# A fused attention, gated feed-forward and spatial-gating kernel: the last token tile made a full, overlapping one, and small attention matmuls given wider streams

## The chip, the cores and the metric

The kernel runs on one core of a Trainium2 chip. The core has a matrix engine (TensorE), a vector engine (VectorE, DVE in the rows), an activation engine (ScalarE, ACT), a general engine (GpSimd, POOL) and a queue engine (SyncE, SP) that starts the transfers between HBM and the core's memory (SBUF). TensorE writes only into PSUM, eight banks of 128 partitions with 512 float32 columns each. The metric is the device time of one launch in microseconds (us).

## The reference

There are three layers behind each other, on 4 batches of 1088 tokens.

1. Linear attention with 4 heads of 32 dimensions. Each q and k row of a head is turned into 64 features: two products with 8x32 matrices S1 and S2 give vectors a and b of 8 numbers, and the features are all products a_i b_j.

```
kv  = einsum('bhsf,bhsd->bhfd', k_p, v);  z = sum(k_p, axis=2)
num = einsum('bhsf,bhfd->bhsd', q_p, kv)
den = einsum('bhsf,bhf->bhs', q_p, z)[..., None] + 1e-06
x   = num / den              # heads side by side: (4, 1088, 128)
```

2. A feed-forward layer with token shift: mixes of x and of x one token earlier go through `w_k` (128x1024), relu and square, then `w_v` (1024x128), times a sigmoid gate from `w_r`.
3. A spatial-gating layer: `w_in` (128x1024) and relu give halves u and v; v is normalised over its 512 features, mixed over tokens by a 1088x1088 matrix plus a bias, multiplied by u, and projected by `w_out` back to 128.

## The kernel before

**Tiling.** The 1088 tokens of a batch are nine tiles: eight of 128 (`NK`) and a last one of 64 (`TAIL`). They are handled in three chunks (`CH`): 384, 384 and 320 tokens, that is three full tiles, three full tiles, and two full tiles with the tail. `rows(t)` gives the rows of a tile. `groups(c)` gives the sets of tiles that one vector instruction can take: one set of three for chunks 0 and 1; for chunk 2 a set of two full tiles and a set with the tail.

**Attention.** `features` (L183) makes three matmuls per chunk, one per tile: the stationary operand is the tile's 128 channels x 128 tokens (64 for the tail), the streamed operand is `Sbd`, a block-diagonal table of 64 columns (4 heads x 16). ScalarE copies the result from PSUM, all of it or the b half, and VectorE or GpSimd forms the 256 products per token (L200 for `KP`, `QP` and batch 1, L208 otherwise). `k_sum` (L217) sums features times v over the nine tiles, for each of two pairs of heads `g`: 128 features stationary, 66 columns streamed (`VP`, two heads of 32 and a column of ones for z). L230 clears the blocks that mix heads with the mask `mk`. `q_turn` (L238) transposes q's features, `q_num` (L255) multiplies them with the masked sums, once per tile and pair, 66 columns streamed into columns of their own, and VectorE divides (L267 to L269). `q_out` (L272) transposes the quotient into `xTs`, and `prep` makes the shifted mixes from it. A plain float32 matmul shows as two instructions in the trace, a float32r matmul and a transpose as one.

**Feed-forward and spatial layer.** `up` (L338) and `down` (L384) run over 96 steps (12 chunks x 8 blocks of 128 hidden features). `mm3` (L108) makes a product from three float32r matmuls of high and low parts with 384 or 320 columns; every second `down` is one plain float32 matmul (L392). `split64` (L119) makes the high and low parts of the weights on VectorE, ScalarE and GpSimd. `v_tile`, `normalise` and `spatial` run the third layer behind it.

**What sets the order.** The program text begins with the weights' and inputs' transfers on SP's queue, 11 warm-up matmuls (L563), the features of k for batch 0, the attention chunk 0 of batch 0, the features and sums of k for batch 1, and then the loop over the 96 steps, in which the other attention chunks are spread by a plan (`plan`, L648; places in `QS`). `behind` issues a call after given instructions; the first weight conversions stand behind the k features and sums (L637, L642), the next behind the first squares of the loop (L693). Inside these bounds a scheduler orders the instructions of each engine by a simulated timeline of its own (L813). Tiles in SBUF and PSUM are shared by name (`sb`, `bank`), so that a transfer into one waits for its last reader: the next v waits for `k_sum`, the next raw weights for a conversion.

Of the kernel before, what the change touches and what calls it, by code (L numbers as in the profile page):

```python
# [21 lines left out]
CH = ((0, 384), (384, 384), (768, 320))  # L22
NCH = len(CH)
NT = 9
NK = 8
TAIL = 64
# [7 lines left out]
VP = 2 * (HD + 1)  # L34
# [28 lines left out]
VW = NH * (HD + 1)  # L63
# [3 lines left out]
def attn_moe_gmlp(ctx: ExitStack, tc: tile.TileContext, qT, kT, va, st, wk, wv, wr, win, wout,  # L67
                  wT, wtail, btail, mu, ident, msk, out):
    nc = tc.nc
    TE, VE, SE, GE = nc.tensor, nc.vector, nc.scalar, nc.gpsimd  # L70
# [16 lines left out]
    def rot(*tags):  # L87
        i = count.get(tags, 0)
        count[tags] = i + 1
        return tags[i % len(tags)]  # L90

    def m(i):
        return f"m{i}"
# [5 lines left out]
        return v if dt == F32 else v.bitcast(dt)  # L99

    idn = sb("idn", [128, 128])
    mk = sb("mk", [128, 8])
    mus = sb("mus", [128, 3])
    half = sb("half", [128, 1])
    ebias = sb("ebias", [128, 1])
# [7 lines left out]
    def copy(dst, src):  # L113
        return SE.activation(out=dst, in_=src, func=AF.Copy)  # L114
# [25 lines left out]
    def flat(r):  # L140
        return r.rearrange("p a b -> p (a b)")
# [8 lines left out]
    def conv64():  # L150
        split64(*pending_raw.pop(0))

    def rows(t):
        return TAIL if t == NT - 1 else 128

    def groups(c):
        return [(0, 3, 128)] if c < 2 else [(0, 2, 128), (2, 1, TAIL)]


    q_s, k_s, v_s, kbd, xTs, kps, qst = {}, {}, {}, {}, {}, {}, {}  # L160
# [13 lines left out]
    def load_v(b):  # L174
        t = sb(rot("xs0H", "xs0L"), [128, NK, NH, HD + 1])
        nc.sync.dma_start(out=t.rearrange("p a b c -> p (a b c)"), in_=va[:, b, :NK * VW])
        t2 = sb(rot("va0", "va1"), [128, NH, HD + 1])
        nc.sync.dma_start(out=t2[:TAIL].rearrange("p b c -> p (b c)"), in_=va[:TAIL, b, NK * VW:])
        v_s[b] = (t, t2)

    outer, k_mask, first = [None], [None], {}

    def features(src, c, dst, pb=4, eng=None, early=False):  # L183
        ab = bank(pb)[:, :192].rearrange("p (t h r) -> p t h r", t=3, h=NH)
        for t in range(3):
            r = rows(3 * c + t)
            TE.matmul(ab[:r, t].rearrange("p h r -> p (h r)"), lhsT=src[:, (3 * c + t) * 128:(3 * c + t) * 128 + r],  # L187
                      rhs=Sbd, start=True, stop=True)
        if eng is None:
            bs = sb(rot("bs0", "bs1"), [128, 3, NH, 8])  # L190
        elif early:
            sab = sb(m(2 + c), [128, 3, NH, 16])
        else:
            sab = sb("sab", [128, 3, NH, 16])
        for t0, n, r in groups(c):
            if eng is not None:
                copy(sab[:r, t0:t0 + n], ab[:r, t0:t0 + n])
                a_ = sab[:r, t0:t0 + n, :, 0:8].rearrange("p t h i -> p (t h) i")
                b_ = sab[:r, t0:t0 + n, :, 8:16].rearrange("p t h j -> p (t h) j")
                outer[0] = eng.tensor_tensor(  # L200
                    out=dst[:r, t0:t0 + n].rearrange("p t (h i j) -> p (t h) i j", h=NH, i=8),
                    in0=a_.unsqueeze(3).to_broadcast([r, n * NH, 8, 8]),
                    in1=b_.unsqueeze(2).to_broadcast([r, n * NH, 8, 8]), op=ALU.mult)
                continue
            copy(bs[:r, t0:t0 + n], ab[:r, t0:t0 + n, :, 8:16])
            a_ = ab[:r, t0:t0 + n, :, 0:8].rearrange("p t h i -> p (t h) i")
            b_ = bs[:r, t0:t0 + n].rearrange("p t h j -> p (t h) j")
            outer[0] = VE.tensor_tensor(  # L208
                out=dst[:r, t0:t0 + n].rearrange("p t (h i j) -> p (t h) i j", h=NH, i=8),
                in0=a_.unsqueeze(3).to_broadcast([r, n * NH, 8, 8]),  # L210
                in1=b_.unsqueeze(2).to_broadcast([r, n * NH, 8, 8]), op=ALU.mult)

    def k_feat(b, c, pb=4, eng=None):
        kp = kps[b, c] = sb((KB1 if b == 1 else ("n0H", "n0L", "n1H"))[c], [128, 3, 256])
# [2 lines left out]
    def k_sum(b, g, ts=range(NT)):  # L217
        if g == 0 and ts[0] == 0:
            kps[b] = bank(3 if b == 1 else 5)
        kv = kps[b]  # L220
        v8 = v_s[b][0].rearrange("p t h c -> p t (h c)")
        v9 = v_s[b][1].rearrange("p h c -> p (h c)")
        for t in ts:
            r = rows(t)
            kp = kps[b, t // 3][:r, t % 3, 128 * g:128 * g + 128]
            vt = (v8[:, t] if t < NK else v9[:r])[:, VP * g:VP * g + VP]
            TE.matmul(kv[:, VP * g:VP * g + VP], lhsT=kp, rhs=vt, start=(t == 0), stop=(t == NT - 1))  # L227
        if g == 1:
            kb = sb(rot("kb0", "kb1"), [128, 2, 2, HD + 1])
            k_mask[0] = VE.tensor_tensor(out=kb, in0=kv[:, :2 * VP].rearrange("p (g h c) -> p g h c", g=2, h=2),  # L230
                             in1=mk[:, 4:6].unsqueeze(1).unsqueeze(3).to_broadcast([128, 2, 2, HD + 1]), op=ALU.mult)
            kbd[b] = kb.rearrange("p g h c -> p g (h c)")

    def q_feat(i):
        qp = qst[i] = sb("n1L", [128, 3, 256])
# [2 lines left out]
    def q_turn(i):  # L238
        c = i % 3
        n = CH[c][1]  # L240
        qp, qt = qst[i], []
        for g in range(2):
            pt = bank(6 + g)
            for t in range(3):
                r = rows(3 * c + t)
                TE.transpose(pt[:, 128 * t:128 * t + r], qp[:r, t, 128 * g:128 * g + 128], idn[:r, :r])  # L246
            q2 = vr(rot(0, 1, 2, 3), CMAX)
            copy(q2[:, :n], pt[:, :n])
            qt.append(q2)
        qst[i] = qt  # L250

    nd_pe, x_copy, x_mu_op = [None], [None], [None]
    nd_last, x_mu, x_turn = [None], [None], [None]

    def q_num(i):  # L255
        b, c = divmod(i, 3)
        qt, kb = qst[i], kbd[b]
        nd = bank(5)[:, :396].rearrange("p (t h c) -> p t h c", t=3, h=NH)
        for t in range(3):
            r = rows(3 * c + t)  # L260
            for g in range(2):
                nd_pe[0] = TE.matmul(nd[:r, t, 2 * g:2 * g + 2].rearrange("p h c -> p (h c)"),  # L262
                                       lhsT=qt[g][:, 128 * t:128 * t + r], rhs=kb[:, g], start=True, stop=True)
        xm = qst[i] = vr(rot(4, 5), CMAX).rearrange("p (t h c) -> p t h c", t=3, h=NH)
        den = sb(rot("de0", "de1"), [128, 3, NH])
        for t0, n, r in groups(c):
            VE.tensor_scalar(out=den[:r, t0:t0 + n], in0=nd[:r, t0:t0 + n, :, HD], scalar1=1e-6, scalar2=None, op0=ALU.add)  # L267
            VE.reciprocal(out=den[:r, t0:t0 + n], in_=den[:r, t0:t0 + n])
            nd_last[0] = VE.tensor_tensor(out=xm[:r, t0:t0 + n], in0=nd[:r, t0:t0 + n, :, 0:HD],  # L269
                             in1=den[:r, t0:t0 + n].unsqueeze(3).to_broadcast([r, n, NH, HD]), op=ALU.mult)  # L270

    def q_out(i):  # L272
        b, c = divmod(i, 3)
        o, n = CH[c]
        if c == 0:
            xTs[b] = sb(f"x{b}", [128, S + 1])
            GE.memset(xTs[b][:, 0:1], 0.0)
        xm = qst.pop(i)
        px = bank(5)
        for t in range(3):  # L280
            r = rows(3 * c + t)
            x_turn[0] = TE.transpose(px[:, 128 * t:128 * t + r], xm[:r, t].rearrange("p h c -> p (h c)"), idn[:r, :r])  # L282
        x_copy[0] = copy(xTs[b][:, 1 + o:1 + o + n], px[:, :n])
        if i == 0:
            a = x_mu[0] = sb(m(1), [128, n])
            x_mu_op[0] = VE.tensor_scalar(out=a, in0=px[:, :n], scalar1=mus[:, 0:1], scalar2=None, op0=ALU.mult)
# [258 lines left out]
        nc.sync.dma_start(out=out[:, b * S + o:b * S + o + n], in_=ob)  # L545


    rawS = sb("rawS", [128, 16, 2], I32)
    nc.sync.dma_start(out=flat(rawS), in_=st.bitcast(I32))
    nc.sync.dma_start(out=mk, in_=msk)  # L550
    load_k(0)
# [10 lines left out]
    for n in range(NWARM):  # L562
# [1 line left out]
    VE.memset(ebias, -896.0 * 2 ** 23)  # L564
    VE.memset(half, -0.5)
    SE.activation(out=warm, in_=half, func=AF.Sigmoid)
    Sl, Ss = sb("Sl", [128, 16]), sb("Ss", [128, 16])
    split64(rawS, 16, None, Sl, Ss)
    Sb = sb("Sbd", [128, NH, 16])
    VE.tensor_tensor(out=Sb, in0=Ss.unsqueeze(1).to_broadcast([128, NH, 16]),  # L570
                     in1=mk[:, 0:NH].unsqueeze(2).to_broadcast([128, NH, 16]), op=ALU.mult)
    Sbd = flat(Sb)
    for t in T2s:
        GE.memset(t.bitcast(F32), 0.0)
# [159 lines left out]
    for b in range(B):  # L734
# [3 lines left out]
        for u, (d, c) in enumerate(order):  # L738
# [78 lines left out]
```

## Time and profile before

| | us |
|---|---|
| median of 3 runs | 487.64 (486.53 to 490.29) |
| the profiled execution | 486.65 |
| its span in the profile | 484.9 |
| TensorE busy (matmul) | 473.9 (98%) |
| VectorE busy | 238.1 (49%) |
| ScalarE busy | 238.8 (49%) |
| GpSimd busy | 190.3 (39%) |

The chain that ended last is TensorE's for 86% of the span, VectorE's for 7%, transfers' for 2%. The profile counts a matmul from its start until its modelled end; since matmuls are pipelined, the pace of a line is read from the chain of waits (length of a piece over its instructions), not from the duration of one.

### The profile page before, as it was taken

The page shows a single profiled execution, that of the slowest core. Times are in us where ns is not written, and L with a number is a line of the kernel's source. Part 1 is how long each engine was busy: PE and PEld are TensorE (multiplying, and loading weights), DVE is VectorE, ACT ScalarE, POOL GpSimd, SP SyncE. Part 2 cuts the span into 40 slices and gives each one's busy share as a digit, 9 for nine tenths or more (in the row PEclk, how much of TensorE's full clock was granted, in tenths as well). Part 3 has the DMA queues.
Part 4 walks back from the last instruction along what each step waited for, and adds up shares of the span by engine and source line. Part 5 has one row for each costly group of instructions (what it writes and reads, how often), then busy time and mean ns, then how long its engine had stood idle before and what let it go on. Part 6 is the DMA issues. An engine that isn't in the chain of part 4 may idle for free.

```text
span 484.9 us, 7337 instructions
## 1 busy us (share of the span) xinstructions
PE 473.9 (98%) x2754; PEld 448.2 (92%) x2754; DVE 238.1 (49%) x452; ACT 238.8 (49%) x577; POOL 190.3 (39%) x248
## 2 busy tenths in 40 slices
PE   7999999899999999999999999999999999999997
PEld 6998788798898889999999999999999999999996
DVE  3525976878866678455572425532225531221221
ACT  2316578888877687766443613333423342411121
POOL 2243755757546468756333612352202342200000
PEclk8557999999999999999999999999999999999999
DMA  7934210011210000012100000000000000100001
GB/s 225 312 106 130 96 47 0 18 49 50 76 32 18 1 1 0 1 48 77 47 18 17 1 15 0 1 1 1 33 15 1 1 1 0 47 0 1 2 0 46
DMA packets 11971, 18.63 MB, mean 38 GB/s; under 512 B 1760, under 2 KB 10528, under 8 KB 11936
## 3 DMA queue, kind: packets, MB, share of 16 engines
q1 hardware_dynamic: 11936, 18.17, 11.9%
q8 instruction: 21, 0.34, 0.3%
q14 instruction: 14, 0.11, 0.1%
HBM read 15.93 MB, written 2.23 MB: 37 GB/s over the span
## 4 chain that ended last, share of the span: by engine, by line
PE 86%; DVE 7%; DMA 2%; ACT 2%; issue 1%; POOL 1%; SPq 1%; DVEq 0%; ACTq 0%; POOLq 0%
PE p L111 65%; PE p L227 5%; PE p L392 4%; PE p L187 3%; PE p L262 2%; DVE w L117 2%; PE p L246 2%; PE p L514 2%; PE p L515 2%; DMA w<-in_qT_dram 1%; PE p L282 1%; DVE w L128 1%; DVE w L124 1%; DMA st<-in_btail_dram 1%; DVE mx L320 1%
## 5 line engine op out<-in xcount | busy, mean ns | idle before, releaser
L519 DVE TENSOR_TENSOR m<-p,m 128x384 f32<-128x384 f32 (+1 forms) x43 | 22.9, 533 | 97.0 <-PE p L515 92.8
L111 PE MATMUL p<-m,k 128*128 128x384 f32 (+1 forms) x288 | 67.5, 353 | 0.4 <-ACT m L114 0.3
L349 POOL TENSOR_TENSOR m<-m 128x384 f32<-128x384 f32 (+1 forms) x48 | 42.2, 884 | 43.6 <-ACT m L346 40.2
L506 ACT ACTIVATE m<-p 128x384 f32<-128x384 f32 (+1 forms) x44 | 20.6, 469 | 77.9 <-PE p L111 76.3
L111 PEld LDWEIGHTS p<-m,k 128*128 128x128 f32 x288 | 49.1, 193 | 3.7 <-ACT m L114 0.5
L111 PE MATMUL p<-w,m 128*128 128x384 f32 (+1 forms) x288 | 52.1, 328 | 0.0
L111 PE MATMUL p<-w,k 128*128 128x384 f32 (+1 forms) x288 | 51.9, 328 | 0.0
L346 ACT ACTIVATE m<-p 128x384 f32<-128x384 f32 (+1 forms) x96 | 43.2, 471 | 16.8 <-PE p L111 16.1
L111 PE MATMUL p<-w,n1H 128*128 128x384 f32 (+1 forms) x192 | 49.2, 332 | 0.1
L111 PEld LDWEIGHTS p<-w,m 128*128 128x128 f32 x288 | 48.1, 188 | 0.4
L111 PEld LDWEIGHTS p<-w,k 128*128 128x128 f32 x288 | 48.0, 188 | 0.4
L111 PE MATMUL p<-w,n0H 128*128 128x384 f32 (+1 forms) x192 | 48.3, 329 | 0.0
L117 DVE TENSOR_TENSOR m<-m,m 128x384 fp32r<-128x384 f32 (+1 forms) x47 | 26.9, 573 | 32.9 <-ACT m L114 27.2
L117 DVE TENSOR_TENSOR w<-m,w 128x384 fp32r<-128x384 f32 (+1 forms) x44 | 33.8, 780 | 18.8 <-ACT w L378 9.6
L111 PEld LDWEIGHTS p<-w,n1H 128*128 128x128 f32 x192 | 34.3, 188 | 1.7 <-DVE x L519 0.5
L392 PE MATMUL p<-w,wvT 128*128 128x384 f32 (+1 forms) x88 | 34.6, 474 | 0.3 <-POOL wvT L687 0.3
L111 PEld LDWEIGHTS p<-w,n0H 128*128 128x128 f32 x192 | 34.1, 188 | 0.6
L460 POOL TENSOR_SCALAR rs<-mv 128x1 f32<-128x1 f32 x34 | 8.6, 254 | 66.3 <-DVE mv L459 65.3
L454 ACT ACTIVATE VR<-p 128x512 f32<-128x512 f32 x34 | 19.7, 597 | 29.7 <-PE p L111 28.4
L111 PE MATMUL p<-w,n1L 128*128 128x384 f32 (+1 forms) x96 | 31.5, 328 | 0.0
L111 PE MATMUL p<-w,n0L 128*128 128x384 f32 (+1 forms) x96 | 31.5, 328 | 0.0
L458 DVE BATCH_NORM_STATS2 bn<-VR 128x6 f32<-128x512 f32 x34 | 23.2, 686 | 14.3 <-ACT VR L454 14.3
(193 smaller groups left out, 1064.6 us busy)
## 6 DMA issues: line engine op xcount, KB each, us to landing
st<-in_wT_dram SPq DMA_DIRECT2D x16, 192.0 KB, 2.4
w<-in_kT_dram SPq DMA_DIRECT2D x8, 192.0 KB, 3.9
w<-in_qT_dram SPq DMA_DIRECT2D x8, 192.0 KB, 4.1
out_dram<-m SPq DMA_DIRECT2D x8, 192.0 KB, 1.9
st<-in_wT_dram SPq DMA_DIRECT2D x8, 160.0 KB, 2.2
xs0H<-in_va_dram SPq DMA_DIRECT2D x2, 528.0 KB, 7.2
xs0L<-in_va_dram SPq DMA_DIRECT2D x2, 528.0 KB, 5.4
w<-in_wk_dram SPq DMA_DIRECT2D x2, 512.0 KB, 5.8
```

The source lines that it names most:

```text
L111: TE.matmul(out_ap, lhsT=l, rhs=r, start=first and n == 0, stop=last and n == 2)
L117: return eng.tensor_tensor(out=L, in0=src, in1=H.bitcast(F32), op=ALU.subtract)
L187: TE.matmul(ab[:r, t].rearrange("p h r -> p (h r)"), lhsT=src[:, (3 * c + t) * 128:(3 * c + t) * 128 + r], rhs=Sbd, start=True, stop=True)
L227: TE.matmul(kv[:, VP * g:VP * g + VP], lhsT=kp, rhs=vt, start=(t == 0), stop=(t == NT - 1))
L246: TE.transpose(pt[:, 128 * t:128 * t + r], qp[:r, t, 128 * g:128 * g + 128], idn[:r, :r])
L346: SE.activation(out=r, in_=hk, func=AF.Relu)
L349: anchor[2] = GE.tensor_tensor(out=sq, in0=r, in1=r, op=ALU.mult)
L392: TE.matmul(vvs[i], lhsT=wvT[:, f // 2], rhs=hls.pop(g), start=f == 0, stop=f == NF - 1)
L454: SE.activation(out=v, in_=pv, func=AF.Relu)
L458: VE.bn_stats(out=bn, in_=v)
L506: SE.activation(out=u, in_=pu, func=AF.Relu)
L519: VE.tensor_tensor(out=u, in0=acc, in1=u, op=ALU.mult)
```

## The change

The last token tile of a batch becomes a full one: it holds the last 128 tokens, 64 of which its neighbour holds too. `cut` gives its place; where transposes write it into a shared PSUM row, `order3` lets it go first, so that its neighbours write over the overlap. In the k sums the rows of the overlap are zero in the v tail (now 128 rows, the values in the last 64), and so is their column of ones. All chunks thus take one instruction per step on VectorE, ScalarE and GpSimd, and `rows` and `groups` go. `Sbd` gets 128 columns, the second 64 of them zero (its mask columns are zero), so that a feature matmul streams 128; the next tile's matmul writes over these. For batches 0 and 2 `k_sum` streams all 132 columns of v for each pair, the mask clears what mixes heads, and `q_num` adds the two pairs up in PSUM with 132 columns each; batches 1 and 3 keep 66. Three small tiles move into shared ones (`rawS`, `Sl`, `Ss`).

```diff
-    mk = sb("mk", [128, 8])
+    mk = sb("mk", [128, 24])
...
+    def order3(c):
+        return (2, 0, 1) if c == NCH - 1 else (0, 1, 2)
+
+    def cut(c, t, o=0):
+        a = CH[c][1] - 128 if t == 2 else 128 * t
+        return slice(o + a, o + a + 128)
...
-        nc.sync.dma_start(out=t2[:TAIL].rearrange("p b c -> p (b c)"), in_=va[:TAIL, b, NK * VW:])
+        nc.sync.dma_start(out=t2.rearrange("p b c -> p (b c)"), in_=va[:, b, NK * VW:])
...
     def features(src, c, dst, pb=4, eng=None, early=False):
-        ab = bank(pb)[:, :192].rearrange("p (t h r) -> p t h r", t=3, h=NH)
+        wide = bank(pb)
+        ab = wide[:, :192].rearrange("p (t h r) -> p t h r", t=3, h=NH)
         for t in range(3):
-            r = rows(3 * c + t)
-            TE.matmul(ab[:r, t].rearrange("p h r -> p (h r)"), lhsT=src[:, (3 * c + t) * 128:(3 * c + t) * 128 + r],
-                      rhs=Sbd, start=True, stop=True)
+            TE.matmul(wide[:, 64 * t:64 * t + 128], lhsT=src[:, cut(c, t, CH[c][0])], rhs=Sbd, start=True, stop=True)
...
+            copy(sab, ab)
...
+        outer[0] = (eng or VE).tensor_tensor(
+            out=dst.rearrange("p t (h i j) -> p (t h) i j", h=NH, i=8),
+            in0=a_.unsqueeze(3).to_broadcast([128, 3 * NH, 8, 8]),
+            in1=b_.unsqueeze(2).to_broadcast([128, 3 * NH, 8, 8]), op=ALU.mult)
...
+        wide = b % 2 == 0
+        w = VW if wide else VP
         for t in ts:
-            r = rows(t)
-            kp = kps[b, t // 3][:r, t % 3, 128 * g:128 * g + 128]
-            vt = (v8[:, t] if t < NK else v9[:r])[:, VP * g:VP * g + VP]
-            TE.matmul(kv[:, VP * g:VP * g + VP], lhsT=kp, rhs=vt, start=(t == 0), stop=(t == NT - 1))
+            kp = kps[b, t // 3][:, t % 3, 128 * g:128 * g + 128]
+            vt = v8[:, t] if t < NK else v9
+            TE.matmul(kv[:, w * g:w * g + w], lhsT=kp, rhs=vt if wide else vt[:, VP * g:VP * g + VP],
+                      start=(t == 0), stop=(t == NT - 1))
...
-            for t in range(3):
-                r = rows(3 * c + t)
-                TE.transpose(pt[:, 128 * t:128 * t + r], qp[:r, t, 128 * g:128 * g + 128], idn[:r, :r])
+            for t in order3(c):
+                TE.transpose(pt[:, cut(c, t)], qp[:, t, 128 * g:128 * g + 128], idn)
...
-                nd_pe[0] = TE.matmul(nd[:r, t, 2 * g:2 * g + 2].rearrange("p h c -> p (h c)"),
-                                       lhsT=qt[g][:, 128 * t:128 * t + r], rhs=kb[:, g], start=True, stop=True)
+                wide = b % 2 == 0
+                o = nd[:, t] if wide else nd[:, t, 2 * g:2 * g + 2]
+                nd_pe[0] = TE.matmul(o.rearrange("p h c -> p (h c)"), lhsT=qt[g][:, cut(c, t)], rhs=kb[:, g],
+                                     start=not wide or g == 0, stop=not wide or g == 1)
...
+    Sb = sb("Sbd", [128, 2 * NH, 16])
+    VE.tensor_tensor(out=Sb, in0=Ss.unsqueeze(1).to_broadcast([128, 2 * NH, 16]),
+                     in1=mk[:, 0:2 * NH].unsqueeze(2).to_broadcast([128, 2 * NH, 16]), op=ALU.mult)
```

## Rows read from the trace of the kernel before

**Rows 1.** The page, the span in 40 slices: TensorE's busy tenths, its granted clock.

```profile
PE   7999999899999999999999999999999999999997
PEclk8557999999999999999999999999999999999999
```

**Rows 2.** Stretches: length; busy us per engine; then granted clock, DMA share, GB/s.

```profile
12.00:24.00 12.00, 12.00 (x55) 11.52 (x55) 6.54 (x14) 4.53 (x11) 2.75 (x2) 0.50 0.94 313
48.00:60.00 12.00, 11.06 (x66) 9.01 (x66) 11.02 (x20) 7.05 (x18) 9.16 (x8) 1.00 0.29 94
```

**Rows 3.** The same table, fine, around the clock's two edges.

```profile
9.40:9.60 0.20, 0.00 (x0) 0.00 (x0) 0.00 (x0) 0.00 (x0) 0.00 (x0) 0.56 1.17 407
43.20:43.40 0.20, 0.20 (x3) 0.08 (x2) 0.08 (x1) 0.20 (x1) 0.20 (x1) 0.50 0.00 0
43.40:43.60 0.20, 0.20 (x2) 0.20 (x2) 0.08 (x1) 0.20 (x2) 0.20 (x1) 0.60 0.00 0
```

**Rows 4.** Timeline: start, length, engine, instruction, idle time before it and its releaser.

```profile
9.88 1.54 PE L187 MATMUL p<-Sbd,w 128*128 128x64 f32 x6 [2.25 <-DMA w<-in_qT_dram]
```

**Rows 5.** Chain of waits, low clock: start, length, line, instructions.

```profile
11.43 3.54 PE p L227 x16
...
16.25 4.85 PE p L227 x20
21.10 1.47 PE p L246 x6
22.57 2.44 PE p L187 x12
25.00 2.76 PE p L262 x12
...
30.32 0.64 PE p L282 x3
30.96 6.88 PE p L227 x30
37.84 2.86 PE p L111 x8
```

**Rows 6.** Chain of waits, full clock: the same lines, and the gated matmul.

```profile
65.72 0.66 PE p L246 x6
66.38 0.65 PE p L187 x6
...
69.77 1.29 PE p L262 x12
...
94.09 1.51 PE p L227 x14
...
103.20 0.65 PE p L392 x2
```

**Rows 7.** Timeline of GpSimd, ScalarE and VectorE between 24 and 42 us.

```profile
24.26 3.11 POOL L200 TENSOR_TENSOR w<-m 128x768 f32<-128x768 f32 x3 [5.05 <-ACT m L114]
...
32.91 0.52 ACT L114 ACTIVATE m<-mx 128x384 fp32r<-128x384 f32 x1 [1.42 <-DVE mx L306]
...
41.80 0.42 DVE L124 TENSOR_SCALAR w<-w 128x512 int32<-128x512 int32 x1
```

**Rows 8.** Batch 0's v: its issue on SP; transfers with us to landing.

```profile
4.00 0.43 SPq L176 DMA_DIRECT2D xs0H<-in_va_dram  x1
...
xs0H<-in_va_dram SPq DMA_DIRECT2D x2, 528.0 KB, 7.2
```

**Rows 9.** Lines by form: tail matmuls, count, busy us, mean ns.

```profile
L187 PE MATMUL p<-Sbd,w 128*64 128x64 f32 x16 | 2.9, 270 | 0.0
...
L262 PE MATMUL p<-kb,VR 128*64 128x66 f32 x16 | 2.2, 240 | 0.0
```

**Rows 10.** Timeline of VectorE, tail instructions of one chunk.

```profile
47.82 0.41 DVE L208 TENSOR_TENSOR n1L<-p,bs 64x256 f32<-64x256 f32 x1
...
60.17 0.28 DVE L269 TENSOR_TENSOR VR<-p,de 64x128 f32<-64x128 f32 x1
```

More of the change, by code (lines that the diff above doesn't have):

```diff
@@ L151, in conv64 @@
         split64(*pending_raw.pop(0))
[L153 to L157, printed above, removed]
+    def order3(c):
[3 more added lines that the diff above has]
+        return slice(o + a, o + a + 128)
     q_s, k_s, v_s, kbd, xTs, kps, qst = {}, {}, {}, {}, {}, {}, {}
@@ L189, in features @@
         if eng is None:
             bs = sb(rot("bs0", "bs1"), [128, 3, NH, 8])
-        elif early:
-            sab = sb(m(2 + c), [128, 3, NH, 16])
-        else:
[L194 to L211, printed above, removed]
@@ new lines, in features @@
+            copy(bs, ab[:, :, :, 8:16])
+            a_ = ab[:, :, :, 0:8].rearrange("p t h i -> p (t h) i")
+            b_ = bs.rearrange("p t h j -> p (t h) j")
+        else:
+            sab = sb(m(2 + c) if early else "sab", [128, 3, NH, 16])
+            copy(sab, ab)
+            a_ = sab[:, :, :, 0:8].rearrange("p t h i -> p (t h) i")
+            b_ = sab[:, :, :, 8:16].rearrange("p t h j -> p (t h) j")
+        outer[0] = (eng or VE).tensor_tensor(
+            out=dst.rearrange("p t (h i j) -> p (t h) i j", h=NH, i=8),
+            in0=a_.unsqueeze(3).to_broadcast([128, 3 * NH, 8, 8]),
+            in1=b_.unsqueeze(2).to_broadcast([128, 3 * NH, 8, 8]), op=ALU.mult)
@@ L222, in k_sum @@
         v9 = v_s[b][1].rearrange("p h c -> p (h c)")
+        wide = b % 2 == 0
+        w = VW if wide else VP
         for t in ts:
-            r = rows(t)
-            kp = kps[b, t // 3][:r, t % 3, 128 * g:128 * g + 128]
-            vt = (v8[:, t] if t < NK else v9[:r])[:, VP * g:VP * g + VP]
-            TE.matmul(kv[:, VP * g:VP * g + VP], lhsT=kp, rhs=vt, start=(t == 0), stop=(t == NT - 1))
+            kp = kps[b, t // 3][:, t % 3, 128 * g:128 * g + 128]
+            vt = v8[:, t] if t < NK else v9
+            TE.matmul(kv[:, w * g:w * g + w], lhsT=kp, rhs=vt if wide else vt[:, VP * g:VP * g + VP],
+                      start=(t == 0), stop=(t == NT - 1))
         if g == 1:
[L229 to L232, printed above, removed]
+            nh = w // (HD + 1)
+            kb = sb(f"kb{b % 2}", [128, 2 * nh, HD + 1])
+            k_mask[0] = VE.tensor_tensor(out=kb, in0=kv[:, :2 * w].rearrange("p (h c) -> p h c", c=HD + 1),
+                                         in1=(mk[:, 8:16] if wide else mk[:, 16:20]).unsqueeze(2)
+                                         .to_broadcast([128, 2 * nh, HD + 1]), op=ALU.mult)
+            kbd[b] = kb.rearrange("p (g h) c -> p g (h c)", g=2)
     def q_feat(i):
@@ L259, in q_num @@
         for t in range(3):
-            r = rows(3 * c + t)
             for g in range(2):
-                nd_pe[0] = TE.matmul(nd[:r, t, 2 * g:2 * g + 2].rearrange("p h c -> p (h c)"),
-                                       lhsT=qt[g][:, 128 * t:128 * t + r], rhs=kb[:, g], start=True, stop=True)
+                wide = b % 2 == 0
+                o = nd[:, t] if wide else nd[:, t, 2 * g:2 * g + 2]
+                nd_pe[0] = TE.matmul(o.rearrange("p h c -> p (h c)"), lhsT=qt[g][:, cut(c, t)], rhs=kb[:, g],
+                                     start=not wide or g == 0, stop=not wide or g == 1)
         xm = qst[i] = vr(rot(4, 5), CMAX).rearrange("p (t h c) -> p t h c", t=3, h=NH)
         den = sb(rot("de0", "de1"), [128, 3, NH])
[L266 to L270, printed above, removed]
+        VE.tensor_scalar(out=den, in0=nd[:, :, :, HD], scalar1=1e-6, scalar2=None, op0=ALU.add)
+        VE.reciprocal(out=den, in_=den)
+        nd_last[0] = VE.tensor_tensor(out=xm, in0=nd[:, :, :, 0:HD],
+                                      in1=den.unsqueeze(3).to_broadcast([128, 3, NH, HD]), op=ALU.mult)
     def q_out(i):
@@ L279, in q_out @@
         px = bank(5)
-        for t in range(3):
-            r = rows(3 * c + t)
-            x_turn[0] = TE.transpose(px[:, 128 * t:128 * t + r], xm[:r, t].rearrange("p h c -> p (h c)"), idn[:r, :r])
+        for t in order3(c):
+            x_turn[0] = TE.transpose(px[:, cut(c, t)], xm[:, t].rearrange("p h c -> p (h c)"), idn)
         x_copy[0] = copy(xTs[b][:, 1 + o:1 + o + n], px[:, :n])
@@ L545, in finish @@
         nc.sync.dma_start(out=out[:, b * S + o:b * S + o + n], in_=ob)
-    rawS = sb("rawS", [128, 16, 2], I32)
+    rawS = sb(m(9), [128, 16, 2], I32)
     nc.sync.dma_start(out=flat(rawS), in_=st.bitcast(I32))
@@ L566, in attn_moe_gmlp @@
     SE.activation(out=warm, in_=half, func=AF.Sigmoid)
-    Sl, Ss = sb("Sl", [128, 16]), sb("Ss", [128, 16])
+    Sl, Ss = sb(m(10), [128, 16]), sb(m(8), [128, 16])
     split64(rawS, 16, None, Sl, Ss)
-    Sb = sb("Sbd", [128, NH, 16])
-    VE.tensor_tensor(out=Sb, in0=Ss.unsqueeze(1).to_broadcast([128, NH, 16]),
-                     in1=mk[:, 0:NH].unsqueeze(2).to_broadcast([128, NH, 16]), op=ALU.mult)
+    Sb = sb("Sbd", [128, 2 * NH, 16])
+    VE.tensor_tensor(out=Sb, in0=Ss.unsqueeze(1).to_broadcast([128, 2 * NH, 16]),
+                     in1=mk[:, 0:2 * NH].unsqueeze(2).to_broadcast([128, 2 * NH, 16]), op=ALU.mult)
     Sbd = flat(Sb)
@@ L776 @@
     va = np.zeros((B, NT * 128, NH, HD + 1), v.dtype)
-    va[:, :S, :, :HD] = v.transpose(0, 2, 1, 3)
-    va[:, :S, :, HD] = 1.0
+    vt = v.transpose(0, 2, 1, 3)
+    va[:, :NK * 128, :, :HD], va[:, :NK * 128, :, HD] = vt[:, :NK * 128], 1.0
+    va[:, -TAIL:, :, :HD], va[:, -TAIL:, :, HD] = vt[:, NK * 128:], 1.0
     wt = moe2_w_spatial.T
@@ L783 @@
     btail[96] = moe2_b_spatial
-    msk = np.zeros((128, 8), np.float32)
+    msk = np.zeros((128, 24), np.float32)
     for h in range(NH):
         msk[32 * h:32 * h + 32, h] = 1.0
-    msk[:64, 4] = 1.0
-    msk[64:, 5] = 1.0
+        msk[64 * (h % 2):64 * (h % 2) + 64, 8 + NH * (h // 2) + h] = 1.0
+        msk[64 * (h % 2):64 * (h % 2) + 64, 16 + h] = 1.0
     host = {
```

## The prediction, made before the changed kernel ran

> **What bounds the kernel now.** I read the row of the granted TensorE clock over the span first. Away from the last slice it is at full speed except in the first tenth [rows 1], and TensorE is busy in nearly every slice. The table of stretches says what that tenth is: from 12 to 24 us TensorE is busy 12.00 of 12.00 us at a granted clock of 0.50, that is at 1.2 instead of 2.4 GHz [rows 2]. The fine table dates the two edges [rows 3]: the clock falls between 9.4 and 9.6 us, with TensorE idle (it waits 2.25 us, to 9.88, for the first chunk of q [rows 4]), and rises between 43.4 and 43.6 us. The reader is to see one low stretch of 34 us, and nothing like it later.
>
> The chain of waits then shows what fills it: TensorE alone, without a pause, on the small float32 matmuls of the first attention steps [rows 5]. A float32 matmul is two instructions here (a features call has 3 matmuls and 6 instructions), so instructions are counted. The feature matmuls (64 columns) take 2.44/12 = 0.203 us each, the sums of k times v (66 columns) 3.54/16 = 0.221, the numerator matmuls (66 columns) 2.76/12 = 0.230. After the rise the same lines take 0.65/6 = 0.108, 1.51/14 = 0.108 and 1.29/12 = 0.108 us [rows 6]. The stretch ends with the first 384-column instructions at 37.84 us [rows 5]; the rise comes 5.7 us behind them. From about 42 us VectorE leads (weight conversions, from the instruction at 41.80 us on [rows 7]; 11.02 of 12.00 us busy in the stretch from 48 [rows 2]), and from about 65 us TensorE again to the end. So time saved ahead of 37.84 us moves all that follows, as long as VectorE's work moves along: its conversions there hang on the first steps of the up projection, and their weights were issued well before.
>
> **The change, part by part.**
>
> *Wider streams, the price.* Feature matmuls go from 64 to 128 streamed columns; the k-v sums and numerators of batches 0 and 2 from 66 to 132; those of batches 1 and 3 stay at 66. The count of instructions does not change. What would 128 columns cost at full clock? The gated 384-column float32 matmul takes 0.65/2 = 0.325 us per instruction, 0.85 ns a column [rows 6], which gives 0.108 for 128 columns and 0.112 for 132: the stream comes out as long as the present pitch, which 64, 66 and 128 columns (the transposes, 0.66/6 = 0.110) all share [rows 6]. I take the pitch of 0.108 to be that of the 128-column stationary load, behind which the stream lies. So 128 columns cost nothing, and 132 cost 4 ns on 144 instructions: 0.6 us, of which about 0.4 lie behind the first stretch. The cover is the stationary load; without it (stream and load one after the other) an instruction would take 0.216. Bounds 0 and 0.108 us each; the transposes, nearest in columns, speak for 0.
>
> *Wider streams, the gain.* The trace shows no 128-column float32 stream of any length while the clock is low, so the effect on the clock is bounded from both sides: none (the clock stays down as now), or never falling. I go by the one rise that the trace shows: 5.7 us after wide instructions began. The wide stream begins again at 9.88 us, so full clock at about 15.6 us. The v data of batch 0 land 7.2 us after their issue at 4.00 us, at 11.2 us, and hold the k-v sum whatever the clock is [rows 8]. Then, from 11.3: 42 instructions (16 and 20 of sums, 6 of features) at 0.221 until 15.6 us makes 19, the other 23 at 0.11 take 2.5 us: 18.1 instead of 21.1 us. Transposes 6 and features 12 at 0.108: 20.05. Numerators, 12: 21.4 instead of 27.8. Then 6 of sums and 6 of features (a repeat of the shapes shown), 3 transposes and 30 narrow sums: 45 x 0.108 = 4.85, up projection from 26.2 instead of 37.84 us: **-11.6 us**. What could be late instead? GpSimd's two feature products of batch 1 take 3.11 us [rows 7]; fed at about 20 us they end at 23.1, and the sums want the last of them at 23.6. The copy that ends the x chain comes 33.43 - 30.96 = 2.5 us after the transposes [rows 5, 7], so 25.5 against 26.2. Both fit by half a microsecond, so an earlier rise is worth little more: with a clock that never falls the sum would end at about 18.1 - 2.2 = 15.9, but GpSimd would hold the up projection to about 24.9, -12.9.
>
> *The first up steps* ran at the low clock: 8 instructions in 2.86 us, half of that back: **-1.4**. The conversions on VectorE start behind them, so this counts too.
>
> *Full tail tile on TensorE.* 16 feature and 16 numerator instructions have 64 stationary columns now [rows 9] and get 128. Between 0 and 0.108 us each, I take half the pitch for half the columns, 0.054: 1.7 us in all, about 1.4 of it behind 26 us where TensorE leads. With the 0.4 above: **+1.8**. The 64-row transposes and sums already load 128 columns: nothing.
>
> *Merged groups on VectorE, ScalarE, GpSimd.* The second instruction of each tail group goes, the first grows. In the stretch that VectorE leads these are a 0.41 us product and a chain that ends with 0.28 us [rows 10]; saved between 0 and 0.7, I take 0.4: **-0.4**. Elsewhere these engines wait for TensorE; nothing. The wider mask product (twice), the mask table of 24 instead of 8 columns and the v tail of 128 instead of 64 rows (33 KB more, four times) stand beside TensorE work or behind the 528 KB of v: nothing; their cover is the work on batch 0 that runs meanwhile, and if it went, 33 KB more would cost 33/528 of those 7.2 us, 0.45 [rows 8].
>
> *Order.* Instructions are ordered by a scheduler's own timeline, which may see wider matmuls as longer and shift some of them. I put +-3 us on it.
>
> Sum: -11.6 - 1.4 + 1.8 - 0.4 = -11.6. The profiled execution took 486.65 us (span 484.9 and 1.75 around it), so 475.0; the median of the runs lies 1.0 above it: **476 us**.
>
> **The rivals.**
>
> *The clock stays down as now.* For it: from 12 to 24 us TensorE was busy all the time, and the clock did not move [rows 2]; no row shows that wide float32 instructions move it. Against it: the one rise followed the change from narrow to wide instructions, and in the mixed stretch from 48 us, with narrow instructions in between, the clock holds at 1.00 [rows 2]. Then only the added terms are left, +1.8 - 0.4 and some 0.4 for four tail instructions at the low clock: 489 us.
>
> The Trainium skill (TensorE: Matmul & The Clock Gate, "What's actually happening") says that the gate follows how busy the engine was lately. If that busy is the busy time of the profile, this change does not touch it and the result is this rival's 489; but the trace disagrees with that reading, since 12.00 busy us of 12.00 left the clock at 0.50.
>
> *The clock rises late, or falls again.* The 30 narrow sums of batch 1 are untouched, 3.2 us of the old kind just ahead of the up projection. If the clock falls in them, the first up steps run slow as now and some of the sums too: -11.6 + 1.8 - 0.4 + 1 = -9.2, 478. If it rises at the numerators (22.6 us) rather than at 15.6, half of the 7 us of delay is lost: 480; a rise at 33 us would leave 485. I put the case at 481.
>
> *Slower: load and stream do not hide each other.* Where the stationary load and a stream of equal length share the array, the pitch may grow. Behind 26 us there are 192 widened instructions (96 feature, 36 sum, 60 numerator), and at 0.216 they cost 192 x 0.108 = +20.7; of the first stretch only the 45 untouched or transposing instructions gain, -4.9, and the first up steps -1.4; with +1.8 - 0.4 that is +15.8: 503. It decides from about 48 ns of growth (some 245 widened instructions at full clock eat 11.7 us), a pitch of 0.156. Against it stands the gated matmul, whose 0.325 has no room for a load in front.
>
> **How the numbers follow.** Forecast 0.60 (own range 471 to 480: the never-falling clock gives 474.7, order and tail terms the rest); late or lost clock 0.19, at 478 to 485; clock down 0.13, at 489; slower 0.08, from 493. Range 471 to 485: the first two cases, 0.79; it leaves out the last two. One per cent, 4.9 us, is about what a measurement of this kernel can tell from no change: faster 0.79, same 0.13, slower 0.08.
>
> **What would show it.** The row of the granted clock should come back to full before 20 us, not at 43 us. The feature lines in the first stretch should go from 0.203 to about 0.11 us, at full clock not over 0.12 for 128 and 132 columns. The first up instruction should stand near 26 us. A clock of 0.50 up to the up projection, or a pitch of over 0.15, would make the forecast wrong; so would an up projection that waits for GpSimd or for a transfer, or conversions on VectorE that do not move forward with it.

## The result, and the profile after

The changed kernel takes 475.4 us (median of 4, 474.82 to 476.61) against 487.29 for the kernel before: a ratio (of the means) of 0.9748, interval 0.9702 to 0.9794. The prediction was 476 us, range 471 to 485. The profiled execution has a span of 473.7 us, 11.2 less.

The page of the changed kernel: busy time of the engines, then the two rows that answer to [rows 1].

```profile
PE 456.4 (96%) x2754; PEld 433.4 (91%) x2754; DVE 235.6 (50%) x433; ACT 236.3 (50%) x569; POOL 189.9 (40%) x247
...
PE   6987999989999999999999999999999999999997
...
PEclk9899999999999999999999999999999999999999
```

The long low stretch is gone: only the second slice shows a dent. TensorE's busy time fell by 473.9 - 456.4 = 17.5 us, more than the span; its idle time (span less busy) rose from 11.0 to 17.3. So 6.3 us of the gain on TensorE were given back as waits. The table of stretches of the changed kernel dates the dent and shows where the waits are (columns as in [rows 2]).

```profile
10.00:12.00 2.00, 1.48 (x11) 1.32 (x12) 0.24 (x2) 0.25 (x1) 0.00 (x0) 0.96 0.99 367
12.00:14.00 2.00, 2.00 (x11) 2.00 (x11) 2.00 (x4) 0.72 (x1) 0.00 (x0) 0.50 1.00 351
14.00:16.00 2.00, 2.00 (x14) 2.00 (x14) 1.93 (x4) 1.06 (x2) 0.00 (x0) 0.69 0.94 315
16.00:18.00 2.00, 2.00 (x21) 2.00 (x20) 0.71 (x3) 0.21 (x2) 1.27 (x1) 1.00 1.04 382
...
30.00:40.00 10.00, 6.87 (x52) 6.26 (x51) 9.23 (x16) 9.28 (x22) 4.62 (x6) 1.00 0.44 131
40.00:50.00 10.00, 8.45 (x50) 6.45 (x49) 8.07 (x14) 4.38 (x12) 6.71 (x7) 1.00 0.28 95
```

From the shares, the clock falls at about 11.8 us and is back at about 15.2, where before it lay low from 9.4 to 43.5 [rows 3]. From 30 to 50 us TensorE is idle for 4.7 of 20 us at full clock while VectorE is busy for 9.23 and 8.07 of 10. The chain of waits of the changed kernel, ahead of the up projection (it answers to [rows 5]):

```profile
11.30 5.97 PE p L219 x36
...
18.43 2.01 DVE w L127
20.46 0.63 ACT w L131
21.09 0.23 ACT m L114
21.32 0.07 issue
21.39 2.98 POOL w L199 x2
24.41 2.89 PE p L219 x24
27.31 1.30 PE p L111 x7
```

The reader is to see that TensorE is no longer alone on it. The sums of batch 0 end at 17.3 us instead of 21.1. Then a conversion step on VectorE took 2.01 us; ScalarE's next conversion step (L131) waited for it, and ScalarE's copy of the batch-1 features stood behind that step in its queue; GpSimd's products started at 21.39, and the k-v sums of batch 1 waited for them until 24.41.

The same stretch in the changed kernel's timeline, TensorE and one VectorE instruction (it answers to [rows 6, 7]):

```profile
18.41 1.50 PE L188 MATMUL p<-Sbd,w 128*128 128x128 f32 x12
...
19.75 1.52 PE L257 MATMUL p<-kb,VR 128*128 128x132 f32 x12
...
21.11 0.83 PE L188 MATMUL p<-Sbd,w 128*128 128x128 f32 x6
...
27.12 1.83 PE L111 MATMUL p<-m,k 128*128 128x384 f32 x9
...
31.27 0.41 DVE L124 TENSOR_SCALAR w<-w 128x512 int32<-128x512 int32 x1
```

From start to start, 12 feature instructions with 128 columns take 19.75 - 18.41 = 1.34 us, 0.112 each; 12 numerator instructions with 132 columns 1.36 us, 0.113 each. The up projection starts at 27.12 instead of 37.77 us (there as here by the start of its first instruction): 10.65 of the span's 11.2 us are won ahead of it.

### The profile page after: what moved, and what is told of

It is laid out like the page before. It is cut to its first block, busy times and chain, and to the rows that moved or that the text cites. A ratio compares the mean times of both kernels' runs of the same rounds, so it can differ in the third digit from the quotient of the medians.

```text
span 473.7 us, 7304 instructions
## 1 busy us (share of the span) xinstructions
PE 456.4 (96%) x2754; PEld 433.4 (91%) x2754; DVE 235.6 (50%) x433; ACT 236.3 (50%) x569; POOL 189.9 (40%) x247
## 4 chain that ended last, share of the span: by engine, by line
PE 71%; DVE 9%; ACT 6%; DMA 5%; POOL 4%; issue 3%; SPq 1%; POOLq 0%; DVEq 0%; ACTq 0%
PE p L111 59%; DMA st<-in_wT_dram 3%; PE p L385 3%; DVE w L117 3%; PE p L219 2%; PE p L257 2%; PE p L507 2%; PE p L508 2%; ACT m L339 2%; DMA xs0H<-in_va_dram 2%; PE p L188 1%; DVE w L127 1%; ACT w L114 1%; DVE m L117 1%; ACT w L371 1%
## 5 line engine op out<-in xcount | busy, mean ns | idle before, releaser
L111 PE MATMUL p<-m,k 128*128 128x384 f32 (+1 forms) x288 | 65.4, 347 | 2.7 <-ACT m L339 2.7
L111 PEld LDWEIGHTS p<-m,k 128*128 128x128 f32 x288 | 47.8, 189 | 6.9 <-ACT m L339 3.7
L455 DVE TENSOR_SCALAR VR<-VR,mv,rs 128x512 f32<-128x512 f32 x34 | 21.1, 621 | 20.4 <-POOL rs L454 20.4
```

The lines of the kernel that those rows point to most:

```text
L111: TE.matmul(out_ap, lhsT=l, rhs=r, start=first and n == 0, stop=last and n == 2)
L455: VE.tensor_scalar(out=v, in0=v, scalar1=mv[:, 0:1], scalar2=rs, op0=ALU.subtract, op1=ALU.mult)
```

## The experiments

"Up" is the start of the up projection, "rest" the span less that; both and TensorE's busy time are from the profiled execution. Ratios are to the kernel before, measured beside each kernel. The profile values of "tail only" stand with its repeat.

| kernel | median us | ratio, interval | up | rest | busy | low clock (start + length, us) |
|---|---|---|---|---|---|---|
| before | 487.3 to 488.2 | | 37.77 | 447.1 | 473.9 | 9.4 + 34.1 |
| changed | 475.4 | 0.9748 (0.9702 to 0.9794) | 27.12 | 446.6 | 456.4 | 11.8 + 3.4 |
| tail only | 489.22 | 1.0042 (1.0009 to 1.0075) | | | | |
| tail only, again | 489.79 | 1.0036 (1.0010 to 1.0061) | 35.65 | 451.8 | 469.6 | 8.1 + 30.7; 59.3 + 3.4 |
| wide only | 484.63 | 0.9917 (0.9887 to 0.9946) | 29.26 | 451.4 | 465.2 | 11.1 + 3.4; 41.9 + 3.4 |
| features only | 478.58 | 0.9801 (0.9757 to 0.9846) | 29.44 | 446.1 | 459.5 | 11.4 + 10.2; 96.7 + 3.4 |
| sums only | 475.81 | 0.9744 (0.9705 to 0.9782) | 27.39 | 447.6 | 457.3 | 8.0 + 6.8; 45.5 + 3.4 |
| before, filled wait | 489.98 | 1.0006 (0.9966 to 1.0046) | 35.23 | 453.5 | 474.1 | 16.2 + 23.9; 91.3 + 3.4 |
| changed, filled wait | 474.11 | 0.9718 (0.9683 to 0.9754) | 27.53 | 445.0 | 457.3 | none |
| early conversion | 475.04 | 0.9734 (0.9701 to 0.9768) | 26.98 | 445.9 | 458.2 | 26.6 + 3.4; 43.6 + 3.4 |
| wide early only | 478.53 | 0.9793 (0.9766 to 0.9820) | 26.37 | 449.8 | 458.6 | 26.2 + 3.4; 94.4 + 3.4 |
| 64-row sums | 476.58 | 0.9761 (0.9733 to 0.9788) | 28.26 | 446.3 | 459.0 | 10.6 + 3.4 |
| all wide | 476.91 | 0.9768 (0.9743 to 0.9793) | 27.33 | 448.3 | 457.3 | 12.2 + 3.4 |
| all three | 475.16 | 0.9731 (0.9706 to 0.9756) | 27.06 | 446.9 | 459.7 | none |

**Which half makes the gain?** Four kernels with parts of the change, first the full tail without wide streams (`tail only`):

```diff
-            TE.matmul(wide[:, 64 * t:64 * t + 128], lhsT=..., rhs=Sbd, start=True, stop=True)
+            TE.matmul(wide[:, 64 * t:64 * t + 64], lhsT=..., rhs=Sbd[:, :64], start=True, stop=True)
...
-        wide = b % 2 == 0        # in k_sum and in q_num
+        wide = False
```

> The change's full tail tile and merged groups, but all streams at 64 and 66 columns as before. Theory A (the gain is the clock, and the clock follows the wide streams): the granted clock stays at 0.50 until the up projection's first matmuls have run for some us, up projection near 37.5 us, time 485 to 489 us. Rival B (the gain is from fewer and merged vector instructions and the order that the scheduler makes of them): 475 to 479 us with the clock low as before.

It took 489.22 us, 0.2 above Theory A's range: the full tail alone gains nothing. The repeat below shows that the clock behaves as before. The wide streams without the full tail (`wide only`; the kernel before, with):

```diff
-            TE.matmul(ab[:r, t].rearrange("p h r -> p (h r)"), lhsT=..., rhs=Sbd, ...)
+            TE.matmul(wide[:r, 64 * t:64 * t + 128], lhsT=..., rhs=Sbd, ...)     # Sbd: 128 columns
...
+        wide = b % 2 == 0        # 132 columns in k_sum and q_num; tail of 64 rows as before
```

> Only the wide streams (128 columns for features, 132 for the sums and numerators of batches 0 and 2); the tail stays 64 rows with instructions of its own. Theory A: clock back at 1.00 by 16 us, up projection near 27 us, 474 to 478 us. Rival B: 484 us or more.

It took 484.63 us, where I expected 474 to 478: a miss, and the time that rival B had named. The clock came back as expected (low for 3.4 us from 11.1), and up moved to 29.26 us, 8.5 earlier, but the rest took 4.3 us longer than before. So the clock theory holds for the first stretch, and the two halves don't add up: +1.8 and -2.8 alone, -11.9 together. On top of the wide streams the full tail, worth nothing alone, is worth 9 us. The tables of stretches from up to the end show where: kernel before, wide only, changed kernel.

```profile
37.77:484.87 447.10, 439.73 (x2603) 415.48 (x2602) 223.85 (x417) 229.56 (x554) 179.63 (x221) 0.99 0.08 24
29.26:480.69 451.43, 442.03 (x2603) 414.47 (x2602) 222.09 (x418) 229.23 (x554) 181.13 (x221) 1.00 0.08 24
27.12:473.74 446.62, 434.09 (x2604) 411.99 (x2603) 219.83 (x401) 227.11 (x548) 179.14 (x221) 1.00 0.08 24
```

Behind up, TensorE is busy for 442.0 us with the small tail and for 434.1 us with the full one; the low stretch at 41.9 us is worth at most 1.7 of these 7.9 us. Then each kind of wide stream by itself, on the changed kernel:

```diff
-        wide = b % 2 == 0
+        wide = False             # features only
```

> The changed kernel with 66 columns for all sums and numerators; only features stream 128. Theory A: of the instructions between 11.3 us and the up projection 66 are features or transposes at best and over 80 are narrow, the 36 sums of batch 0 in one run; the clock falls in that run and comes back late or not before the up projection: 480 to 487 us. If a few wide instructions are enough to hold the clock: 474 to 477. Rival B: 475 to 479.

```diff
-            TE.matmul(wide[:, 64 * t:64 * t + 128], lhsT=..., rhs=Sbd, ...)
+            TE.matmul(wide[:, 64 * t:64 * t + 64], lhsT=..., rhs=Sbd[:, :64], ...)   # sums only
```

> The changed kernel with a table of 64 columns for the features; sums and numerators of batches 0 and 2 stream 132. Theory A: the 36 sums of batch 0 bring the clock back by about 16 us as in the changed kernel; the 12 narrow features behind them (1.3 us) and the narrow sums of batch 1 may lower it again: 474 to 481 us. Rival B: 475 to 479.

478.58 and 475.81 us. The first is below Theory A's range and within rival B's, the second within both. With wide features alone the clock lay low through the 36 narrow sums, for 10.2 us, and up moved to 29.44; with wide sums alone it was low for 6.8 us and up was at 27.39, as in the changed kernel. Either brings most of the gain, with the low stretch shorter where the longest run, the sums, is wide. Fewer vector instructions, the rival, are in all three tail kernels and gain nothing in the first; what they add beside wide streams, these kernels do not separate.

**Why does the full tail alone gain nothing?** The first kernel once more, for its profile.

> The tail-only kernel once more, for its profile: the timed runs gave 489.2 us, 1.8 above before, though its trace should lack the 64-row matmuls. In the traces of before and of the wide-only kernel, an instruction that changes the matmul's shape from 128x128 to 64 rows or 64 columns starts 0.205 us behind its neighbour instead of 0.112, and the change back costs 0.15 to 0.20. Theory A: TensorE busy falls by some 4 to 6 us against before, and waits (VectorE-led stretch, or a longer or second low stretch of the clock) take it back; time 486 to 490 us. Rival: TensorE's busy time does not fall, the full tile is no gain on TensorE at all.

The page of `tail only`, repeated: busy time, and the clock over the span.

```profile
PE 469.6 (96%) x2754; PEld 446.5 (92%) x2754; DVE 236.7 (49%) x433; ACT 237.1 (49%) x569; POOL 191.9 (39%) x247
...
PEclk8559999999999999999999999999999999999999
```

TensorE's busy time is 4.3 us below before, though tail tiles have twice the rows or columns; the span is 2.5 us above, so its idle time rose by 6.8. The clock is low as long as before, and once more at 59 us. Theory A held: the full tail is cheaper on TensorE, and waits took all of it.

**What does a 64-row tile cost?** The changed kernel, with 64 rows in the tail of the sums alone (the rows left out are zero in v):

```diff
         for t in ts:
...
+            if t == NK:
+                kp, vt = kp[TAIL:], vt[TAIL:]
```

> The changed kernel, but the k-v sums use only the 64 lower rows of the tail tile (the upper 64 are zero in v), so that these matmuls alone have 64 rows again: 8 groups of two instructions. Theory from the pace in the trace of before (0.205 us into such a group, 0.161 to 0.216 inside, 0.202 out of it, instead of 0.112): 0.24 to 0.29 us more for each group, TensorE busy 1.9 to 2.3 us more, time 475.5 to 478 us. Rival (rows are free, as the prediction had it for these sums): no more busy time.

The same stretch of the timeline in the changed kernel (all 128 rows), at full clock:

```profile
16.41 0.61 PE L219 MATMUL p<-xs0H,n1H 128*128 128x132 f32 x4
16.86 0.39 PE L219 MATMUL p<-va,n1H 128*128 128x132 f32 x2
17.09 0.83 PE L188 MATMUL p<-Sbd,w 128*128 128x128 f32 x6
```

and with 64 rows in the tail of the sums:

```profile
16.54 0.61 PE L221 MATMUL p<-xs0H,n1H 128*128 128x132 f32 x4
17.09 0.49 PE L221 MATMUL p<-va,n1H 64*128 64x132 f32 x2
17.50 0.71 PE L188 MATMUL p<-Sbd,w 128*128 128x128 f32 x4
```

From the first start to the third: 0.68 us with 128 rows, 0.96 with 64, for the same six instructions. The change of shape costs 0.09 to 0.10 us going in (four starts take 0.55 instead of 0.45), and 0.18 for the tail's two instructions and the way out (0.41 instead of 0.23). The page agrees: 8 such groups at 0.28 us make 2.2 us, and busy time is 2.6 us above the changed kernel.

```profile
PE 459.0 (97%) x2754; PEld 435.1 (92%) x2754; DVE 236.0 (50%) x433; ACT 236.9 (50%) x569; POOL 190.6 (40%) x247
```

The median is 476.58, 1.2 above the changed kernel, with overlapping intervals: the cost on TensorE is shown, its share of the time is within the noise.

**Did the wait or the narrow streams lower the clock?** 14 matmuls on zeros, into an unused bank, while TensorE waits for q:

```diff
+    def fill():
+        for n in range(14):
+            TE.matmul(wp, lhsT=zero[:, :128], rhs=zero, start=n == 0, stop=n == 13)
+    behind(k_pe, fill)            # k_pe: the last feature matmul of k, batch 0
     q_feat(0)
```

In the kernel before:

> The kernel before, with 14 extra 384-column matmuls on zeros into an unused bank while TensorE waits for q (7.6 to 9.9 us); nothing else. It asks whether the idle wait or the narrow streams lower the clock. Theory A (narrow streams do not hold it): the clock is full through 10 us, falls within the narrow run after it and stays low until the up projection; 484 to 488 us. Rival (the idle wait alone loses it, narrow streams would hold a full clock): clock full all along, up projection near 26 us, 476 to 479 us.

The kernel before with the filled wait, stretches:

```profile
10.00:12.00 2.00, 1.45 (x13) 1.25 (x11) 0.07 (x1) 0.00 (x0) 0.00 (x0) 1.00 0.96 334
12.00:14.00 2.00, 2.00 (x18) 1.86 (x17) 1.74 (x5) 0.47 (x2) 0.00 (x0) 1.00 0.95 312
14.00:16.00 2.00, 2.00 (x18) 1.93 (x17) 1.74 (x4) 1.66 (x4) 0.04 (x1) 1.00 0.97 360
16.00:18.00 2.00, 0.95 (x6) 0.81 (x6) 1.81 (x4) 0.16 (x2) 1.24 (x1) 0.56 1.04 364
18.00:20.00 2.00, 2.00 (x12) 2.00 (x10) 0.80 (x3) 1.64 (x4) 0.00 (x0) 0.50 1.02 358
```

The fill carries the full clock through the wait and 4.7 us into the narrow sums, which run from 11.53 to 16.15 us; then it falls and stays low until 40.1 us. Another wait of TensorE (to 17.20 us) begins near the fall, so here is the same table, fine:

```profile
16.00:16.20 0.20, 0.16 (x2) 0.02 (x1) 0.01 (x1) 0.16 (x2) 0.20 (x1) 1.00 1.14 352
16.20:16.40 0.20, 0.00 (x0) 0.00 (x0) 0.20 (x1) 0.00 (x0) 0.20 (x1) 0.59 0.90 329
```

From the share of 0.59, the clock fell at 16.24 us, when this wait had lasted less than 0.1 us. Ahead of it lay 4.6 us of narrow instructions without a pause. So it is the narrow run, and not this wait, that the fall follows. The median did not move: 489.98 us, 2 above Theory A's range; in the profiled execution the rest took 6.4 us longer than before, with a second low stretch at 91 us and other waits. Its timed executions differ: three with a mean granted clock of 0.985 to 0.986 took 483.4 to 485.7 us, six with 0.971 to 0.976 took 488.9 to 490.6.

One thing does not fit. The kernel before also has timed executions with a nearly full clock: of the 46 measured beside the kernels here, seven have a mean of 0.993 to 0.996, where 0.964 goes with the low stretch of 34 us, and they took 488.0 to 489.4 us, no less than the others (485.8 to 490.6). `tail only` has three such (0.990 to 0.995; 488.5 to 493.2 us). There is no trace of them. Either the fall is missing from their clock readings, or a full clock without wide streams does not bring the gain; the runs do not settle it. In the profile of the kernel before, the pace follows the granted clock: the sums of one line take 0.221 us at the low level and 0.108 at full clock [rows 5, 6]. In the changed kernel:

> The changed kernel with the same 14 extra matmuls. If they hold the clock through the wait, the 3.4 us low stretch from 11.8 us goes and TensorE's early steps end 1.7 us sooner; GpSimd's products of batch 1, which the k-v sums already wait for at 24.4 us, and VectorE from 31 us on would take most of it back: theory 474 to 475.5 us. Rival: early TensorE time still moves the end one for one: 473.7 us or less.

The clock is full throughout, and the median is 474.11. Up is not earlier, at 27.53: GpSimd's products are on the chain (three in a row, 5.11 us, until 24.79 us). The theory held, but the difference of 1.3 us to the changed kernel lies inside the intervals.

**Is VectorE the bound from 30 us on?**

```diff
     prep_0 = list(prep_L) + PG * nd_pe0
+    behind(list(prep_L), conv64)
...
     for n in range(3):
-        plan(R0[n], conv_first)
+        if n:
+            plan(R0[n], conv_first)
```

> The changed kernel with the first w_v conversion started right behind the mix for the first up projection instead of behind the first squares of the loop, that is on a VectorE that is idle from 28 to 30.5 us. Theory (VectorE's conversions lead from 31 to 48 us and TensorE's 6 us of extra waiting there come from them): 472 to 474.5 us. Rival (the waits there come from the chain through ScalarE and GpSimd): 475 to 477 us.

475.04 us, the rival's range and not the theory's: the time did not move. The conversion did (26.7 instead of 31.3 us), and the idle time of TensorE in the table of stretches fell from 3.13 to 0.58 us between 30 and 40 us; but in this execution the clock fell twice more, at 26.6 us within the narrow sums of batch 1 and at 43.6. What of the 2.5 us would stay with a full clock, it does not show.

**Does width cost anything later, and is it needed there?** Features narrow again behind the first stretch, `wide = b == 0` for the sums and numerators:

```diff
+        cols = 128 if early_stage[0] else 64
...
+            TE.matmul(wide[:, 64 * t:64 * t + cols], lhsT=..., rhs=Sbd[:, :cols], start=True, stop=True)
...
-        wide = b % 2 == 0
+        wide = b == 0
```

> The changed kernel with wide streams only ahead of the loop of 96 steps and for batch 0's sums; features after that stream 64 columns again, batch 2's sums and numerators 66. Theory (width costs nothing at full clock, since both widths start 0.112 us apart in the traces, and only the first stretch gains): 474.5 to 477.5 us, no difference from the changed kernel beyond what another order of instructions makes. Rival (the later wide streams cost TensorE time, the predicted 0.4 to 20 us): clearly below the changed kernel's 475.4, 473 or less. Third: later wide streams are needed to hold the clock: over 478, with low stretches behind 60 us.

478.53 us, in the range of the third case; but its interval overlaps the changed kernel's, so the 3.1 us between the medians are likely and not certain. Busy time rose by 2.2 us though fewer columns were streamed, and the clock fell twice, once behind 60 us (at 94.4). That the later wide streams are needed is not shown by this alone. The narrow sums of batch 1 in this kernel, timeline:

```profile
23.57 0.66 PE L221 MATMUL p<-xs0L,w 128*128 128x66 f32 x4 [0.58 <-POOL w L201]
24.06 0.39 PE L221 MATMUL p<-va,w 128*128 128x66 f32 x2
24.29 1.95 PE L221 MATMUL p<-xs0L,w 128*128 128x66 f32 x16
26.07 0.54 PE L221 MATMUL p<-va,w 128*128 128x66 f32 x2
26.37 3.23 PE L111 MATMUL p<-m,k 128*128 128x384 f32 x9
```

and its table of stretches:

```profile
24.00:26.00 2.00, 2.00 (x21) 2.00 (x19) 1.41 (x2) 0.66 (x2) 1.83 (x2) 1.00 1.04 380
26.00:28.00 2.00, 2.00 (x10) 2.00 (x9) 1.37 (x3) 0.00 (x0) 0.00 (x0) 0.54 0.59 125
```

Here the clock falls at 26.2 us, after 2.6 us of 66-column instructions without a pause. A wait of 0.58 us for GpSimd stands ahead of them. The changed kernel has the same wait (until 24.41 us) ahead of the same run, and its clock did not fall, so this wait alone does not explain the fall; what made the difference stays open. The nine up instructions behind it take 3.23 us instead of 1.83.

**All batches wide, and all together.** The odd batches' masked sums placed in a row that is free at that time:

```diff
-        wide = b % 2 == 0
+        wide = True
...
-            kb = sb(f"kb{b % 2}", [128, 2 * nh, HD + 1])
+            kb = sb("kb0", ...) if b % 2 == 0 else vr(6, 264).rearrange("p (h c) -> p h c", c=HD + 1)
```

> The changed kernel with 132 columns for the sums and numerators of batches 1 and 3 too. The changed kernel's clock was full through the narrow sums of batch 1 in its profile, but fell within them in the profile of the early-conversion kernel. Theory: no low stretch between 16 and 30 us, otherwise nothing to gain: 474 to 476 us. Rival: 66 columns are needed there (132 cost something): over 477 us.

476.91 us (span 475.6), between the two ranges: no fall in the sums of batch 1, as expected, but no gain, 1.5 us above the changed kernel with overlapping intervals. And with the fill and the early conversion:

> The changed kernel with all three: extra matmuls in the wait for q, the first w_v conversion right behind the first mix, 132 columns everywhere. Expected 472 to 474 us if the three small gains (1.3, 0.4 and 0 us in the medians so far) add up; 474 to 476 if VectorE and GpSimd give them back.

475.16 us, clock full throughout: the small gains do not add up. No version beats the changed kernel by more than the measurement tells; the lowest median is that with the filled wait, 474.11.

## Why the prediction was right, step by step

**The first stretch: right in cause and size, by luck in the date of the rise.** The forecast had the clock back at 15.6 us, 5.7 us behind the start of wide instructions; it was 15.2. But it had the low level from before q on, and the clock fell only at 11.8 us, when wide instructions were already running; in the kernel with early wide streams only it did not fall at all ahead of 26 us. So the delay of 5.7 us is not what the runs show, and 15.2 agrees by luck. Sums until 18.1 us forecast, 17.3 measured; numerators done at 21.4, measured 21.1; up at 26.2, measured 27.12. The missing 0.9 us is the late one that I had named, GpSimd, but by more than I allowed: its pair of products ended at 24.4 us, not at 23.1, since ScalarE's copy stood behind a conversion step that waited for VectorE. I had checked GpSimd's length and not ScalarE's queue. The four part kernels show that the cause is the wide streams: without them up stays at 35.65 us, with them it lies at 27.39 to 29.44. In the profiled executions they act through the clock: pace and granted clock change together. Whether the clock is all that they act through, the seven executions named above leave open.

**The price of width: right.** At full clock 128 columns start 0.112 us apart, 132 columns 0.113, and 66 columns (26.07 - 24.29)/16 = 0.111 in the narrow run above. My 0.108 for the pace was a little short, the 4 ns for 132 columns 1 ns. The rival of load and stream behind each other is out.

**The first up steps, -1.4: wrong.** From up to the first conversion on VectorE it takes 31.27 - 27.12 = 4.15 us, before 41.80 - 37.77 = 4.03. The nine instructions did run faster (1.83 us at full clock), but the chain of waits goes from there through ScalarE (28.70 to 30.37 us) to VectorE, and does not start sooner for it.

**The full tail on TensorE, +1.8: wrong sign.** I priced 64 stationary columns at half the pitch, and took 64 rows to cost what 128 do. Both cost more than a full tile: the change of shape takes about 0.09 us on the way in and 0.04 to 0.09 on the way out. Busy time fell by 4.3 us in the tail-only kernel, and rose by 2.6 with 8 groups put back (there are 32 in all: 8 of features, 8 of sums, 8 and 4 of transposes, 4 of numerators). With wide streams the full tail was worth 9 us of time. By the forecast's own terms the wide streams without it come to about 475 us (487.6 - 11.6 - 1.4 + 0.4); they took 484.6. So the forecast gave the whole gain to the wide streams, and its total is right in part by luck.

**Waits, which I had at nothing: wrong by 6 us the other way.** Of 17.5 us that TensorE no longer works, 6.3 came back as idle time. From 30 to 50 us, where VectorE leads, TensorE is idle for 4.7 us; in the kernel before, the same 20 us behind up have 1.45 us, so 3.2 were added there:

```profile
40.65:60.65 20.00, 18.55 (x110) 15.71 (x109) 18.08 (x34) 14.12 (x35) 12.35 (x11) 0.93 0.34 108
```

The two errors cancel, which is luck: the rest behind up is 446.6 us against 447.1, where the forecast terms -1.4 + 1.8 - 0.4 made 0.

**Order, +-3 us: too small.** Over the kernels tried, with nearly the same work behind up, the rest lies between 445.0 and 453.5 us. The kernel before with 14 matmuls on zeros added took 6.4 us longer there. Part of it are low stretches of 3.4 us, each worth at most half of that; the waits between the engines differ as well. What makes the wide-only kernel's rest 4.3 us longer than that of the kernel before stays open. By the rows above, 2.3 us of it are TensorE's busy time and 2.0 waits. The clock does not explain it: the wide-only kernel has one low stretch of 3.4 us there, and the kernel before has 5.8 us of its long one (37.77 to 43.56).

Of the Trainium skill (TensorE: Matmul & The Clock Gate, "What's actually happening"): that the gate follows how busy the engine was lately is again not what the profile's busy time shows: in the kernel before with the filled wait, the clock fell at 16.24 us behind 4.6 us of busy time without a pause.

## What to carry to other kernels

Look at the granted clock before counting instructions: where TensorE is busy without a pause and the clock is low, streams of more columns can be worth more than streams of fewer. Compare the pace of narrow and wide instructions at full clock: where they start equally far apart, as here with 66 to 132 columns, the added columns are free, even columns of zeros. A small tile is not cheap for being small: count the changes of shape around it, and try a full tile that overlaps its neighbour. And test the halves of a change both alone and together: here one half gained nothing and the other 2.8 us, and both together 11.9.

## What the runs showed of the hardware that I had not expected

- Float32 instructions with a 128x128 stationary operand start 0.111 to 0.113 us apart with 66, 128 or 132 columns at 2.4 GHz.
- Between 128x128 and 64-row shapes TensorE loses time: 0.96 instead of 0.68 us for the six instructions shown, 0.10 of it on the way in, 0.18 inside and on the way out.
- The granted clock fell to half behind 4.6 us (16.24 us, before with the filled wait) and 2.6 us (26.2 us, wide early only) of unbroken narrow instructions, and under the latter run in the changed kernel's profile it did not.
